# k and q of the first batch in runs of nine tokens, q's landmarks by products with a 0/1 matrix, and q turned behind the landmark scores

## The chip, the core and the metric

One core of a Trainium2 chip runs the kernel: TensorE (products), VectorE, ScalarE, GpSimd (POOL) and the DMA queues of SyncE (SP) and POOL. The metric is the device time of one execution in microseconds. The kernel before takes 811.49 us, the median of three runs from 810.85 to 811.83.

## The reference

Attention by landmarks, then two feed-forward layers. For each batch (4) and head (8), with S = 576 tokens, D = 64 and m = 32 landmarks of 18 tokens each:

```python
q_lm = q.reshape(B, H, m, S // m, D).mean(axis=3)
k_lm = k.reshape(B, H, m, S // m, D).mean(axis=3)
A, Bm, C = sm(q, k_lm), sm(q_lm, k_lm), sm(q_lm, k)      # softmax of scaled scores
Z = Bm.T / (norm1(Bm) * norminf(Bm) + 1e-06)
for _ in range(6):
    Z = 2 * Z - Z @ Bm @ Z
x = A @ Z @ C @ v                                        # (B, H, S, D) -> (2304, 512)
h = x @ w_in;  g = max(h, 0) + alpha * min(h, 0);  y = g @ w_out
h = y @ w_in2; g = h * clip(h + 3, 0, 6) / 6;      out = g @ w_out2
```

The weights arrive as 64-bit floats and are made 32-bit in the kernel. The tolerance asks for float32 accuracy, so many products run in three passes over a high and a low part.

## The kernel before, in words

The program has three parts. The **opening** computes the attention of batch 0 by itself. The **main loop** runs the first layer over eight blocks of tokens (two of each batch), 16 steps of 128 hidden features each, with the attention of the next batch and the conversion of weights between them. The last part runs the second layer over three blocks of tokens.

In the opening the order on TensorE, VectorE, ScalarE and SP is the order of the program text (`manual_schedule(engines=set(first))`, line 763); each engine takes its instructions in that order and waits for what each needs. In the main loop only TensorE and SP are ordered by hand, and a scheduler places the rest.

The order of the opening is written out in `attention(b, bank, lat, early, ...)` with `lat` = 0:

- Lines 317 to 330: SP issues k (`load_long`), q and v. `load_long` (line 251) makes one transfer of the last 64 tokens of all heads (64 partitions, runs of 256 bytes) and then `parts` transfers of the first 512 tokens (128 partitions, four tokens or 1 KB a run). k and q have four parts of two heads each. Then `early(0)` issues the first weights.
- `transposed_long` (line 294): for each pair of heads, products with the identity turn the tokens into columns, one ScalarE copy brings 512 columns to SBUF, and VectorE sums 18 columns at a time into a landmark (line 312). k goes through it first, then q. `kT` and `qT` hold the turned k and q, `kT[:, :, S:]` and `qlm` the landmarks; `bdk` is k's landmarks as a block matrix.
- `compared` (line 354): products of q's landmarks with k and k's landmarks, halves of the columns, for even and odd heads (`g`). `most_b`, `exp_b`, `most_c`, `bias_c`, `exp_c`: maxima on VectorE and exponentials on ScalarE, for B and C.
- `blocks`, `norms`: B normalised and its norms. `turned_c`, `turned_rest`: C's exponentials turned. `product`: C times v, into `x0` beside B.
- `scores` (line 428): A's scores for two tiles of tokens, in three parts: products, maximum, subtraction with exponential. `normalised` and `turned` finish A.
- `inverse` (line 503): six iterations. In each, 16 small products, a ScalarE copy and a VectorE sum, whose results the next iteration's products read. Behind each iteration the list `fill` names what else is issued there. A number n stands for `early(n)` and `joins(1)`. `warm(n)` puts n filler products on TensorE, whose results nobody reads.
- `early` (line 741) takes pieces of weights: ScalarE converts the high and the low words of a piece (`words_of`, line 195), 256 columns at a time for the first 16 pieces of `w_in`, then 512 columns of `w_out`, where POOL takes the low words. `joins` puts the two together on VectorE (`joined`, line 212).
- Line 783 on: `project(0, 0, ...)` multiplies the attention's last factor `bd` into the first weights, in two halves, and splits the result. With it the main loop can start. `emitted` counts the pieces that are begun, and the main loop's `LEAD` (line 1137) follows from it: `max(2, emitted[0] + 1)`, with `emitted[0]` the words of `w_out` begun.

A PSUM bank is taken by `bank(...)` from a ring of six in the opening, or by `two(...)` from a ring of two; a product that writes a bank waits until the bank's last reader is done.

## Time and profile before

| | us |
|---|---|
| median of 3 runs (lowest, highest) | 811.49 (810.85, 811.83) |
| the profiled execution: time, and span from first to last instruction | 808.85, 807.0 |
| busy in the span: TensorE, VectorE, ScalarE, POOL | 789.3, 588.2, 455.4, 215.2 |
| the opening, up to the start of the first projection | 37.53 |
| granted clock of TensorE over the span | 1.000 of 2.4 GHz |

Times are microseconds from the first instruction. PE is TensorE's products, PEld its weight loads, DVE is VectorE, ACT ScalarE. A product in 32-bit floats appears as two instructions. "Busy" of PE includes the filler products; products are pipelined and the ends of theirs are modelled. L307 is line 307 of the kernel, and `tp<-ident,rk` says that `tp` was written from `ident` and `rk`.

### The profile page before, as it was taken

How to read it: one execution, taken by the hardware profiler on the slowest of the kernel's cores; microseconds unless marked ns; L12 is line 12 of the kernel's file. 1: busy time of each engine (PE TensorE's matmuls, PEld its weight loads, DVE VectorE, ACT ScalarE, POOL GpSimd, SP SyncE). 2: the span in 40 equal slices, each digit the busy share in tenths (PEclk: the TensorE clock that was granted, in tenths of full speed). 3: DMA queues.
4: the chain of work that ended last, by engine and by line, in shares of the span. 5: the costliest groups of instructions: out<-in, count | busy, mean ns of one | idle time of the engine just before them, and what ended most of it. 6: DMA issues, size and time to landing. Idle time of an engine off the chain costs nothing.

```text
span 807.0 us, 16974 instructions
## 1 busy us (share of the span) xinstructions
PE 789.3 (98%) x6439; PEld 734.3 (91%) x6439; DVE 588.2 (73%) x1198; ACT 455.4 (56%) x987; POOL 215.2 (27%) x291
## 2 busy tenths in 40 slices
PE   9898998999999999999999999999999999999997
PEld 5476897888989989899999999999999999999997
DVE  4797776678856779566895587994677994677962
ACT  4785455676556676566773455752455741555541
POOL 0555003253423533344650232000223000322000
PEclk9999999999999999999999999999999999999999
DMA  9999006777386974369645777777867687677761
GB/s 270 408 414 287 19 32 178 276 228 232 108 246 216 311 229 141 125 205 346 216 156 195 296 267 293 269 281 254 319 231 276 257 300 247 248 268 269 259 229 59
DMA packets 90529, 190.91 MB, mean 237 GB/s; under 512 B 37184, under 2 KB 64336, under 8 KB 83792
## 3 DMA queue, kind: packets, MB, share of 16 engines
q1 hardware_dynamic: 80912, 151.55, 54.9%
q0 software_dynamic: 9536, 38.28, 13.4%
q8 instruction: 51, 0.84, 0.4%
q14 instruction: 30, 0.25, 0.1%
HBM read 146.81 MB, written 42.99 MB: 235 GB/s over the span
## 4 chain that ended last, share of the span: by engine, by line
PE 87%; DVE 5%; ACT 3%; DMA 2%; issue 1%; SPq 0%; DVEq 0%; ACTq 0%
PE acc L134 21%; PE l L134 20%; PE qa L1090 15%; PE h L134 12%; PE qb L1090 7%; PE acc L845 2%; PE wp L698 2%; PE tp L283 2%; PE sa L435 2%; PE sc L359 1%; PE psr L510 1%; DMA raw<-in_moe_w_in_dram 1%; DMA yr<-y_d 1%; ACT raw L202 1%; DMA rk<-in_k_dram 1%
## 5 line engine op out<-in xcount | busy, mean ns | idle before, releaser
L134 PE MATMUL acc<-gs,wout 128*128 128x288 f32 (+1 forms) x1344 | 205.4, 299 | 0.0
L134 PEld LDWEIGHTS acc<-gs,wout 128*128 128x128 f32 x1344 | 186.0, 188 | 3.1 <-issue 1.3
L134 PE MATMUL l<-yf,st 128*128 128x384 f32 x1008 | 175.5, 336 | 0.1
L134 PEld LDWEIGHTS l<-yf,st 128*128 128x128 f32 x1008 | 174.6, 188 | 0.5 <-DVE g L1037 0.5
L1090 PE MATMUL qa<-st,s 128*128 128x256 f32 x1008 | 147.3, 282 | 0.0
L1090 PEld LDWEIGHTS qa<-st,s 128*128 128x128 f32 x1008 | 132.1, 191 | 0.0
L134 PE MATMUL h<-a,w 128*128 128x288 f32 (+2 forms) x768 | 129.6, 304 | 1.7 <-DVE t L827 1.1
L128 ACT CAST s<-g 128x384 fp32r<-128x384 f32 x168 | 84.4, 512 | 79.1 <-PE qb L1090 51.2
L134 PEld LDWEIGHTS h<-a,w 128*128 128x128 f32 x768 | 108.5, 188 | 19.3 <-issue 4.4
L129 DVE TENSOR_TENSOR s<-g,s 128x384 fp32r<-128x384 f32 x168 | 88.9, 555 | 19.3 <-ACT s L128 16.4
L904 POOL TENSOR_TENSOR raw<-raw 128x128 f32<-128x128 f32 x128 | 73.6, 587 | 85.3 <-DMA raw<-in_moe_w_in_dram 34.8
L1051 POOL TENSOR_TENSOR p<-p,p 128x384 f32<-128x384 f32 x24 | 26.5, 1105 | 235.9 <-ACT p L1046 235.9
L1090 PE MATMUL qb<-st,s 128*128 128x256 f32 x504 | 87.4, 282 | 0.0
L827 DVE SCALAR_TENSOR_TENSOR t<-t,beta,h 128x288 f32<-128x288 f32 (+1 forms) x112 | 57.7, 515 | 34.7 <-ACT t L826 34.0
L826 ACT ACTIVATE t<-h 128x288 f32<-128x288 f32 (+2 forms) x120 | 49.6, 414 | 58.8 <-PE h L134 57.9
L1090 PEld LDWEIGHTS qb<-st,s 128*128 128x128 f32 x504 | 72.0, 191 | 0.0
L129 DVE TENSOR_TENSOR gs<-t,gs 128x288 fp32r<-128x288 f32 (+1 forms) x112 | 56.0, 500 | 19.8 <-ACT gs L128 19.5
L128 ACT CAST gs<-t 128x288 fp32r<-128x288 f32 (+1 forms) x112 | 48.9, 437 | 27.9 <-DVE t L827 26.5
L908 POOL DMA_DIRECT2D w_d<-fb x32 | 21.2, 661 | 66.9 <-DVE fb L129 37.7
L206 POOL TENSOR_SCALAR raw<-raw 128x512 int32<-128x512 uint32 x16 | 29.5, 1842 | 26.9 <-DMA raw<-in_moe_w_out_dram 26.0
L1036 ACT ACTIVATE ta<-l,three 128x384 f32<-128x384 f32 x24 | 14.0, 582 | 38.4 <-PE l L134 35.2
L845 PE MATMUL acc<-gs,raw 128*128 128x256 f32 x128 | 31.7, 385 | 0.0
(206 smaller groups left out, 1034.8 us busy)
## 6 DMA issues: line engine op xcount, KB each, us to landing
st<-w_d SPq DMA_DIRECT2D x48, 896.0 KB, 6.0
st<-w_d SPq DMA_DIRECT2D x42, 1024.0 KB, 5.9
w_d<-fb POOLq DMA_DIRECT2D x32, 512.0 KB, 4.1
w_d<-fa POOLq DMA_DIRECT2D x32, 384.0 KB, 3.3
raw<-in_moe_w_in_dram SPq DMA_DIRECT2D x16, 512.0 KB, 10.7
raw<-in_moe_w_out_dram SPq DMA_DIRECT2D x16, 512.0 KB, 11.3
raw<-in_moe_w_in_dram SPq DMA_DIRECT2D x64, 128.0 KB, 4.8
raw<-in_moe_w_out_dram SPq DMA_DIRECT2D x64, 128.0 KB, 4.6
```

The costliest lines, as they stand in the source:

```text
L128: nc.scalar.copy(hi, src),
L129: rest.tensor_tensor(out=lo, in0=src, in1=hi.bitcast(F32), op=ALU.subtract),
L134: nc.tensor.matmul(ps, lhsT=lhs(x), rhs=rhs(y), start=first and i == 0, stop=last and i == 2, **kw)
L206: nc.gpsimd.tensor_scalar(out=low, in0=low.bitcast(U32), scalar1=0.9374 * 2.0 ** -29, scalar2=None, op0=ALU.mult)
L283: nc.tensor.transpose(ps[:, j, :n], raw[:n, t, j * P:(j + 1) * P], ident[:n, :n])
L826: nc.scalar.activation(out=t, in_=h, func=AF.Relu, scale=-1.0),
L827: nc.vector.scalar_tensor_tensor(out=gs[:, 0] if plain else t, in0=t, scalar=beta[:, kk:kk + 1], in1=h, op0=ALU.mult, op1=ALU.add),
L845: nc.tensor.matmul(acc, lhsT=words[kk][:, ms], rhs=gs[:, 0], start=at_ == 0, stop=at_ == NK - 1)
L904: nc.gpsimd.tensor_tensor(out=y[:, o], in0=p, in1=q_, op=op)
L908: nc.gpsimd.dma_start(out=to, in_=f.bitcast(F32))
L1051: nc.gpsimd.tensor_tensor(out=p7, in0=p7, in1=p5, op=ALU.add)
L1090: nc.tensor.matmul(to[t], lhsT=s[:, y, t * P:(t + 1) * P], rhs=w[:, kp % 4, :, z], start=kp == 0 and m == 0 and t != 1, stop=kp == NU - 1 ...
```

## The change

k and q of batch 0 come by `load_runs`: each head's 576 tokens lie over 64 partitions, nine tokens (2304 bytes) in each, and two pairs of heads share the 128 partitions. A transfer brings two heads to one half of the partitions; there are four each for k and q. `turned_run` turns three of the nine tokens of two pairs of heads by six products with the identity, and `placed` copies them to their columns, which lie nine apart. k is turned that way at once, with every second copy on VectorE, and its landmarks are summed in two sums over 1152 columns. q's landmarks come from products of q with `windows`, a matrix of zeros and ones whose column l has ones at the two partitions that hold landmark l's 18 tokens; nine products for each pair are summed in PSUM, and one ScalarE copy brings all to SBUF. q itself is turned later: one half behind the landmark scores, the other half around C's product with v, the last third of that half behind the first iteration. A's first scores move into the iterations, the scores and maxima are ordered by even and odd heads, and there are fewer fillers. Pieces of weights in the iterations and just ahead of them: 12, where there were 15. `rs6` takes the buffer of `eb`.

```diff
+    HP = P // 2
+    RUN = S // HP
...
+    windows = const.tile([P, 2 * M], F32, name="windows")
+    nc.vector.tensor_reduce(
+        out=windows, in_=ident.rearrange("p (c r) -> p c r", r=W // RUN), op=ALU.add, axis=AX.X
+    )
...
+    def load_runs(src, b, nm):
+
+        raw = sb.tile([P, NTI * H * D], F32, tag="raw", name=nm, bufs=2)[:, :NP * RUN * D]
+        raw = raw.rearrange("p (i g c) -> p i g c", i=2, g=NG)
+        for i in range(2):
+            for a in range(2):
+                h = NG * (2 * i + a)
+                nc.sync.dma_start(
+                    out=raw[a * HP:(a + 1) * HP, i], in_=src[b, h:h + NG].rearrange("g (p t) d -> p g (t d)", t=RUN)
+                )
+        return raw.rearrange("p i g (t d) -> p i g t d", t=RUN)
...
-        def transposed_long(raw, xt, lm):
...
+        def both_g(ps, raw, i, t, rhs, **kw):
+            for g in range(NG):
+                nc.tensor.matmul(ps[64 * g:64 * g + 64], lhsT=raw[:, i, g, t], rhs=rhs, **kw)
+
+        def turned_run(raw, i, x, ps):
+            for t in range(3):
+                both_g(ps[:, t * P:(t + 1) * P], raw, i, 3 * x + t, ident, start=True, stop=True)
+            return ps
+
+        def placed(xt, i, x, ps, copy):
+            to = xt[:, 2 * i:2 * i + 2, :S].rearrange("q a (p t) -> q t a p", t=RUN)
+            copy(to[:, 3 * x:3 * x + 3], ps[:, :3 * P].rearrange("q (t a p) -> q t a p", t=3, a=2))
...
-            raws["k", b] = load_long(k, b, "rk", NP)
+            raws["k", b] = load_runs(k, b, "rk")
...
-        rq = load(q, b, "rq") if lat else load_long(q, b, "rq", NP)
-        turn = transposed if lat else transposed_long
+        rq = (load if lat else load_runs)(q, b, "rq")
...
-        for _ in turn(raws["k", b], kT, kT[:, :, S:]):
-            yield True
-        if lat:
+            rk = raws["k", b]
+            for i in range(2):
+                for x in range(3):
+                    placed(kT, i, x, turned_run(rk, i, x, bank("tp")), nc.vector.tensor_copy if x == 1 else nc.scalar.copy)
+                nc.vector.tensor_reduce(
+                    out=kT[:, 2 * i:2 * i + 2, S:],
+                    in_=kT[:, 2 * i:2 * i + 2, :S].rearrange("p a (l r) -> p a l r", r=W), op=ALU.add, axis=AX.X,
+                )
...
-        for _ in turn(rq, qT, qlm):
-            yield True
...
+            lm = bank("lm")
+            for i in range(2):
+                for t in range(RUN):
+                    both_g(lm[:, i * 2 * M:(i + 1) * 2 * M], rq, i, t, windows, start=t == 0, stop=t == RUN - 1)
+            nc.scalar.copy(qlm, lm[:, :NP * M].rearrange("p (j l) -> p j l", j=NP))
...
-            for hf in (1, 0):
-                for g in range(NG):
+            for g in range(NG):
+                for hf in range(2):
                     compared(g, hf)
-            a0 = scores([0, 1])
-            next(a0)
-            most_b(range(NG))
             for g in range(NG):
+                most_c(g, 0)
+                most_b([g])
+                most_c(g, 1)
+                bias_c(g)
                 exp_b(g)
-            for g in range(NG):
-                most_c(g, 1)
-                most_c(g, 0)
-                bias_c(g)
                 exp_c(g)
+            q0 = [turned_run(rq, 0, x, (two, two, bank)[x]("tp")) for x in range(3)]
             blocks()
-            warm(3)
             turned_c(0)
             norms()
             turned_c(1, nc.vector.tensor_copy)
             turned_rest()
+            for x in range(3):
+                placed(qT, 0, x, q0[x], nc.scalar.copy)
             c_scale()
-            drain(product())
+            q1 = [turned_run(rq, 1, 0, two("tp"))]
+            product_ = product()
+            next(product_)
+            q1.append(turned_run(rq, 1, 1, two("tp")))
             consts()
-            warm(6)
-            next(a0)
+            for x in range(2):
+                placed(qT, 1, x, q1[x], nc.scalar.copy)
             early(1)
+            a0 = scores([0, 1])
             n0, t0 = normalised([0, 1]), turned([0, 1])
             early(1)
             joins(1)
-            fill = [[2, a0], [2, 1], [2, n0], [1, n0], [2, 1], [t0, 1], [1]]
+            fill = [[2, 1], [a0, 2], [a0, 1, a0], [1, n0], [n0, 1], [t0, 1], [1]]
             for i, _ in enumerate(inverse()):
+                if i == 0:
+                    placed(qT, 1, 2, turned_run(rq, 1, 2, bank("tp")), nc.scalar.copy)
...
-                warm((5, 5, 4, 4, 3, 3, 6)[i])
+                warm((3, 1, 4, 4, 3, 3, 6)[i])
```

## Rows read from the trace of the kernel before

**Rows 1.** The page: busy time and share of the span of each engine.

```profile
PE 789.3 (98%) x6439; PEld 734.3 (91%) x6439; DVE 588.2 (73%) x1198; ACT 455.4 (56%) x987; POOL 215.2 (27%) x291
```

**Rows 2.** Busy time by stage: stretch, its length, busy time of each engine, clock, DMA.

```profile
25.30:38.40 13.10, 11.88 (x151) 5.24 (x150) 9.88 (x29) 10.92 (x37) 8.38 (x5) 1.00 1.02 406
41.60:55.10 13.50, 12.73 (x86) 10.28 (x87) 12.97 (x26) 12.49 (x24) 7.70 (x5) 1.00 1.02 413
55.10:67.50 12.40, 10.77 (x78) 8.48 (x77) 12.23 (x32) 9.03 (x19) 9.83 (x6) 1.00 1.08 375
```

**Rows 3.** The chain of waits, opening: start, length, what held the end.

```profile
3.20 5.57 DMA rk<-in_k_dram
...
10.62 3.71 PE tp L307 x64
14.35 0.59 ACT qT L311
...
14.97 0.77 DVE qlm L312
...
30.16 0.32 ACT raw L202
```

**Rows 4.** TensorE's timeline, from A's first scores to the first projection: start, length.

```profile
16.95 2.00 PE L435 MATMUL sa<-bdk,qT 128*128 128x64 f32 x16
...
23.94 1.47 PE L767 MATMUL idle<-idle 128*128 128x512 bf16 x6
25.34 0.53 PE L510 MATMUL psr<-nx 32*32 32x96 f32 x16
...
37.53 0.79 PE L698 MATMUL wp<-win,bd 64*32 64x256 f32 x16
```

**Rows 5.** k's transfers in the first 20 us: the first issue, all landings.

```profile
L258 SPq DMA_DIRECT2D rk<-in_k_dram x1: 750/750/750, 0.7 to 0.7; - x1
...
DMA to landing us min/median/max: 3.0/3.2/5.6
```

**Rows 6.** Table by stage, transfers: the last two columns are DMA share and GB/s.

```profile
7.20:8.20 1.00, 1.00 (x20) 0.84 (x18) 0.80 (x2) 0.64 (x2) 0.00 (x0) 1.00 1.23 199
9.00:10.40 1.40, 1.40 (x21) 1.09 (x19) 0.75 (x1) 0.57 (x2) 0.00 (x0) 1.00 1.09 348
11.00:12.50 1.50, 1.50 (x32) 1.50 (x30) 0.51 (x2) 0.59 (x1) 0.58 (x2) 1.00 1.22 179
17.00:25.00 8.00, 7.38 (x120) 5.39 (x118) 5.72 (x24) 4.67 (x19) 0.00 (x0) 1.00 1.03 410
```

**Rows 7.** Durations: two rows of TensorE's timeline, then groups by line (busy, mean ns).

```profile
10.55 3.77 PE L307 MATMUL tp<-ident,rq 128*64 128x128 f32 x64
55.83 0.68 PE L435 MATMUL sa<-bdk,qT 128*64 128x64 f32 x8
...
L202 ACT ACTIVATE raw<-raw 128x256 f32<-128x256 f32 x15 | 6.5, 435 | 0.0
...
L311 ACT COPY qT<-tp 128x512 f32<-128x512 f32 x4 | 2.3, 587 | 1.8 <-PE tp L307 1.8
L300 ACT COPY qT<-tp 128x256 f32<-128x256 f32 x1 | 0.4, 378 | 0.0
L443 DVE TENSOR_TENSOR epc<-sa,ma 128x512 f32<-128x512 f32 x1 | 0.7, 684 | 0.0
L444 ACT ACTIVATE epc<-epc 128x512 f32<-128x512 f32 x1 | 0.6, 613 | 0.0
```

**Rows 8.** Weight loads of TensorE that waited, 38.8 to 70 us; POOL's waits there.

```profile
42.25 0.11 PEld L767 LDWEIGHTS <-idle 128*128 128x128 bf16 x2 [1.11 <-DVE w L129]
...
47.62 0.77 PEld L134 LDWEIGHTS h<-a,w 128*128 128x128 f32 x6 [0.84 <-DVE raw L217]
...
67.42 0.20 PEld L465 LDWEIGHTS atp<-ident,epc 64*128 64x128 f32 x2 [1.84 <-issue]
...
POOL raw L206 <- DMA raw<-in_moe_w_out_dram: 8.4, 4, 3.7
```

## What I expect, and why

> **What bounds the kernel now.** The page comes first: TensorE is busy for 98% of the span [rows 1], so work taken off another engine is worth something only where TensorE waits. The table by stage says where that is: from 25.3 to 38.4 us TensorE shows 11.88 of 13.1 us, but much of that is filler products, and ScalarE has 10.92; from 41.6 to 67.5 us VectorE is busy for 0.96 to 0.99 of the time and ScalarE for 0.93, then 0.73 [rows 2]. The change touches the opening alone, and everything behind about 70 us is a queue of products that starts later or earlier as a block. So the question is when the opening hands over. The chain of waits gives its order: k lands at 8.77, q is turned until 14.33, copied until 14.94, and its landmarks are summed until 15.74 [rows 3]. From there a chain of scores, exponentials, C's product with v and six iterations leads to the first projection at 37.53 [rows 4].
>
> I count from 15.74, the end of q's landmarks, and sum against the profiled execution: 807.0 of span and 1.85 around it, 808.85. It stands 2.64 under the median of 811.49, so the sum's difference is put on the median. A measurement tells a difference from none at about 0.2%, 1.6 us.
>
> **The transfers.** Before, k and q came in ten transfers (two tails of 256-byte runs, eight of 1 KB runs). After, eight, each of 64 partitions x 2 heads x 2304 bytes = 294,912 bytes. SP issues two fewer, and the transfers behind them keep their order. No row shows a transfer to half the partitions in long runs, so I bound it. The first transfer, 131,072 bytes, was issued at 0.73 and landed 3.0 us later [rows 5]; at about 0.2 MB per us it moved for 0.65, so the first byte's way and receipt end at 3.1, and the n-th new transfer lands at 3.1 plus n times its duration. Best: the 410 GB/s of the weights' 4 KB runs over all partitions [rows 6], 0.72 each, last q at 8.9. Worst: half of it, 205 GB/s, 1.44 each, last q at 14.6. The nearest rows are the two stretches in which a 64-partition tail was in flight, 199 and 179 GB/s against 348 between them [rows 6]. Their packets are small, so they are no proof, but they lie at the bad end.
>
> The Trainium skill, SBUF — State Buffer, section "Can I just issue two DMAs to hit both halves?", speaks against the change: partitions 0 to 63 reach only half of the DMA's ports, and two transfers, one to each half, gain 6% over one. Its figure of 196 GB/s for 64 partitions would make 1.50 us of each, an estimate, and 1.4 us more in the sum below; the rate of rows 6 for long runs would make it 2.8 less. The low rates beside the tails agree with the page, as far as they go.
>
> **Until q's landmarks are there.** k's turning is 2 x 9 x 2 = 36 products. Each is two instructions (64 stood for the 32 before), at 3.77/64 = 0.059 us [rows 7]: 4.25 us. The landmark products of q are again 36, with the same weight load of 64 columns and half the columns streamed; the row with that load and 64 columns is 0.68 for 8, (0.68 - 0.27)/7 = 0.059 [rows 7]. So 4.25 again, where q's turning cost 3.77 and 0.46. Behind the last product stand 0.27 of its tail and one copy of about 0.27, instead of a copy of 0.59 and a sum of 0.77 [rows 3]. If the transfers are fast, TensorE sets the time: it starts when k's first half is in, 3.1 + 2 x 0.72 = 4.5, and ends at 4.5 + 8.5 + 0.5 = 13.5, a gain of 2.2. If they are slow, the last half of q sets it: 14.6 + 2.1 + 0.5 = 17.2, a loss of 1.5. I take three quarters of the way to the slow end, by the tails' rows: **+0.6**. k's two sums over 1152 elements (about 1.4 by the 0.68 that VectorE takes for 512, rows 7) and its six copies run while TensorE works on q, so they cost nothing; without that cover the second sum's 1.4 would stand on the path. The new sum for the 0/1 matrix stands in VectorE's idle time at 2 us, and costs nothing either.
>
> **From there to the first iteration.** Maxima and exponentials go head pair by head pair now; I count no gain from that, because the norms' chain of small operations stands behind both orders. What is paid: ScalarE now copies three groups of q, 384 columns each. Between 0.38 for 256 and 0.59 for 512 [rows 7] that is 0.48, or 0.39 from start to start. The fourth group of 12 instructions (0.71) needs the bank that the first copy frees, and stands ahead of C's product on TensorE: 0.48 + 0.71. Behind the product another 0.71 stands where six fillers stood, 1.47 [rows 4]: -0.76. So the first iteration's product, 25.34 - 15.74 = 9.6 behind the landmarks before [rows 4], moves to 10.0: **+0.4**.
>
> **In the iterations.** ScalarE's queue decides here: a weight piece is two conversions, 0.32 each from start to start, 0.65 [rows 3], and each iteration's small copy stands behind those ahead of it. Step by step, as differences of the distance from one iteration's product to the next:
> first to second: two copies of q (0.78) join the two pieces ahead of the evacuation, and the six fillers no longer cover that, +1.1;
> second to third: a copy (0.39) and three pieces, for two pieces and the exponential (0.61), +0.5;
> third to fourth: two pieces for three, -0.65;
> fourth to fifth: maximum 0.68, join, subtraction 0.68 and exponential 0.61 [rows 7] now stand in one chain ahead of the copy; about 2.6 for 1.6, +1.0;
> fifth to sixth: sum and reciprocal of A, +0.45.
> **+2.4** in all. Fifteen pieces were converted ahead of the first projection, twelve are after. The 16 products of A's scores move from under the exponentials into the second iteration; their 2.0 [rows 4] lies beside ScalarE's copy and three pieces, 2.3, and would stand on the path without them. The scratch that takes eb's buffer costs nothing, since eb's last reader is ten microseconds back by then.
>
> **Behind the start.** The three pieces, 3 x 0.65 = 1.95 of ScalarE, go where it has 12.49 of 13.5 us busy [rows 2]: between 0 and 1.95, I take the middle, **+1.0**. In that lies, too, that no word of w_out is begun in the opening any more, so that the lead falls from three words to two and VectorE joins each word right behind POOL. On the other side TensorE's loads wait there four times, for VectorE's or ScalarE's backlog: 1.11, 0.84, again 0.84, and 1.84 [rows 8], 4.6 in all. Conversions follow landings, and POOL waited 8.4 us for weights there [rows 8]; a later start meets more of them done. Between 0 and 4.6; I take the last wait and a little, **-1.9**, because the other three stand behind projections that move with the start.
>
> **Sum:** 0.6 + 0.4 + 2.4 + 1.0 - 1.9 = +2.5: 811.35 in a profiled execution, 814.0 as a median. The copies write with a step of nine words; the nearest rows are conversions with a step of two words, 0.435 for 256 against 0.378 for a plain copy [rows 7], so at the worst some 0.08 on each of six copies, +0.5. The likeliest case's own range goes from 813.0, with transfers halfway between their ends (-0.35 for +0.6), to its far end, rival 3.
>
> **Rivals.**
> 1. Full rate, and no more. The transfers run like those to all partitions, because consecutive ones go to different halves. For it: only small packets were seen slow. Sum: -2.2 + 2.8 + 1.0 - 1.9 = -0.3, 811.2, no difference that can be measured.
> 2. Full rate, and the weights behind come sooner too, the side of faster. With q in at 8.9, where TensorE still turned it until 14.33 [rows 3], each weight tile behind it in SP's queue lands some four microseconds sooner; POOL's 8.4 us of waits go, VectorE joins sooner, and all four of TensorE's waits vanish: -2.2 + 2.8 + 1.0 - 4.6 = -3.0, 808.5. It decides from where the gains ahead of the landmarks and in these waits exceed 3.8 + 1.6 = 5.4 together. Against it: between 41.6 and 55.1 ScalarE is full by its own work [rows 2], which landings don't shorten.
> 3. Slow transfers and nothing absorbed, the far end of the forecast: 1.5 + 2.8 + 1.95 + 0.5 = +6.8, 818.3. For it: rows 6; against it: TensorE's wait of 1.84.
>
> **How the numbers follow.** The forecast with its far end has 0.50, rival 1 has 0.28, rival 2 has 0.22. So slower 0.50, same 0.28, faster 0.22. The range goes from 809.0, which leaves out about half of rival 2, to 817.5, which leaves out the far end.
>
> **What would show it.** Right: q's last transfer lands at 13 to 14.6 with about 200 GB/s while k and q come; the copy of q's landmarks ends near 16.3; the first and second iteration's products stand 2.7 apart; the first projection starts near 41. Wrong: 350 GB/s and more ahead of 9 us (rival 1 or 2); the landmark products at under 0.04 us each; iterations as close as before, because ScalarE's copies find idle time; or, with a late first projection, TensorE's wait at 67 gone and the later blocks on time.

## The result, and the profile after

The changed kernel takes 817.04 us (median of 6 executions, 815.04 to 820.5), the kernel before 811.09 beside it (810.49 to 811.83): ratio 1.0087, 95% interval 1.007 to 1.0104 (the quotient of the two medians is 1.0073). It is slower by 5.95 us, where +2.5 was forecast. The profiled executions stand 816.03 against 808.85, spans 814.2 against 807.0, so +7.2 there; the terms below are taken from these two. Executions of one kernel differ by up to 6.6 us (the kernel before, 808.82 to 815.39 in one session), in part with the mean of their granted clock (0.992 to 1.0), which is why a median and a profiled execution are kept apart here.

The page's first part [rows 1] shows nothing: TensorE's busy time has moved by 0.3 us.

```profile
PE 789.6 (97%) x6502; PEld 737.2 (91%) x6502; DVE 588.2 (72%) x1196; ACT 457.9 (56%) x988; POOL 212.0 (26%) x291
```

The table by stage of the changed kernel, from its own marks (stretch, length, busy time of each engine, clock, DMA share and GB/s) [rows 2, 6]:

```profile
5.00:10.00 5.00, 3.83 (x36) 3.86 (x38) 0.85 (x1) 0.85 (x1) 0.00 (x0) 1.00 1.04 227
...
26.45:42.01 15.56, 12.85 (x158) 6.89 (x157) 10.48 (x29) 11.72 (x35) 10.08 (x7) 1.00 1.03 409
```

While k and q come, the transfers move 227 GB/s. The stretch from the first iteration's product to the first projection took 12.19 us before (25.34 to 37.53, rows 4); it takes 15.56, and TensorE, ScalarE and VectorE all show idle time in it.

The chain of waits of the opening (start, length, what held the end) [rows 3]:

```profile
5.45 8.46 DMA rq<-in_q_dram
14.04 1.28 PE lm L314 x36
...
22.22 0.75 ACT qT L323
23.02 0.88 PE tp L314 x12
...
26.14 1.43 ACT qT L323 x2
...
29.50 0.50 ACT qT L323
```

q's last transfer now holds the chain until 13.91, the landmark products follow in 1.28, and three times ScalarE's copies of q stand in the chain. TensorE's timeline [rows 4], the six iterations' products and the first projection:

```profile
26.45 0.83 PE L532 MATMUL psr<-nx 32*32 32x96 f32 x16
...
29.35 0.57 PE L532 MATMUL psr<-nx 32*32 32x96 f32 x16 [0.50 <-ACT nx L559]
...
32.54 0.53 PE L532 MATMUL psr<-nx 32*32 32x96 f32 x16 [0.48 <-DVE nx L562]
...
33.97 0.53 PE L532 MATMUL psr<-nx 32*32 32x96 f32 x16
...
36.55 0.53 PE L532 MATMUL psr<-nx 32*32 32x96 f32 x16 [1.08 <-DVE nx L562]
...
38.31 0.53 PE L532 MATMUL psr<-nx 32*32 32x96 f32 x16 [0.47 <-DVE nx L562]
...
42.01 0.79 PE L725 MATMUL wp<-win,bd 64*32 64x256 f32 x16
```

Before, these stood at 25.34, 26.99, 29.23, 31.28, 32.84, 34.06 and 37.53. The first comes 1.11 us late, the projection 4.48: three quarters of that arise inside the iterations. Two groups by line between 5 and 42 us (busy, mean ns) give the price of what was added:

```profile
L323 ACT COPY qT<-tp 128x384 f32<-128x384 f32 x6 | 4.6, 879 | 0.0
...
L314 PE MATMUL lm<-windows,rq 128*64 128x64 f32 x72 | 2.5, 223 | 0.7 <-DMA rq<-in_q_dram 0.7
```

And the weight loads that waited behind the start [rows 8]:

```profile
46.73 0.11 PEld L794 LDWEIGHTS <-idle 128*128 128x128 bf16 x2 [1.11 <-DVE w L131]
...
52.49 0.77 PEld L136 LDWEIGHTS h<-a,w 128*128 128x128 f32 x6 [0.85 <-DVE gs L854]
55.85 0.30 PEld L136 LDWEIGHTS h<-a,w 128*128 128x128 f32 x2 [1.04 <-ACT w L130]
...
73.51 0.20 PEld L487 LDWEIGHTS atp<-ident,epc 64*128 64x128 f32 x2 [1.84 <-issue]
```

The waits of 1.11, 0.84 and 1.84 of before are all still there, and one of 1.04 for ScalarE is new. The load at 73.51 stood at 67.42: +6.09. From there the same VectorE operations of both kernels, set side by side, are +6.09 at 118 us of before, +5.04 at 157, about that until 570, and +7.1 at the end. So 1.05 comes back between 118 and 157, where TensorE was busy for 35.89 of 40 us before and is for 37.46 now (by stage):

```profile
120.00:160.00 40.00, 37.46 (x410) 31.96 (x409) 27.41 (x59) 24.16 (x56) 11.56 (x18) 1.00 0.57 174
```

The last 2.07 is a wait far behind the change (TensorE's timeline, then VectorE's):

```profile
587.74 2.53 PE L136 MATMUL l<-yf,st 128*128 128x384 f32 x13 [2.07 <-DVE g L1064]
```
```profile
581.02 0.96 DVE L996 TENSOR_TENSOR t<-yr 128x768 f32<-128x768 f32 x1 [1.91 <-DMA yr<-y_d]
```

A transfer of y landed 8.6 us behind its issue, 7.1 before. This is hardly the change's own: the same wait is 0.7 to 1.4 us in the profiles of seven of the twelve kernels below, and 0.2 or less in the other five. Of the kernel before there is one profile, without it, so that it never has this wait is not shown.

### The profile page after: what moved, and what is told of

It reads as the page before. It is cut to its first block, busy times and chain, and to the rows that moved or that the text cites. A ratio compares the mean times of both kernels' runs of the same rounds, so it can differ in the third digit from the quotient of the medians.

```text
span 814.2 us, 17094 instructions
## 1 busy us (share of the span) xinstructions
PE 789.6 (97%) x6502; PEld 737.2 (91%) x6502; DVE 588.2 (72%) x1196; ACT 457.9 (56%) x988; POOL 212.0 (26%) x291
## 4 chain that ended last, share of the span: by engine, by line
PE 86%; ACT 4%; DVE 4%; DMA 3%; issue 1%; SPq 1%; DVEq 0%; ACTq 0%
PE acc L136 20%; PE l L136 20%; PE qa L1117 15%; PE h L136 12%; PE qb L1117 7%; PE acc L872 3%; PE wp L725 2%; PE sa L457 2%; PE tp L301 2%; DMA raw<-in_moe_w_in_dram 1%; DMA yr<-y_d 1%; ACT raw L208 1%; DMA rq<-in_q_dram 1%; PE sc L381 1%; PE psr L532 1%
## 5 line engine op out<-in xcount | busy, mean ns | idle before, releaser
L131 DVE TENSOR_TENSOR gs<-t,gs 128x288 fp32r<-128x288 f32 (+1 forms) x112 | 55.8, 498 | 19.6 <-ACT gs L130 19.1
L212 POOL TENSOR_SCALAR raw<-raw 128x512 int32<-128x512 uint32 x16 | 27.0, 1687 | 23.0 <-DMA raw<-in_moe_w_out_dram 22.1
```

What stands on the lines that cost most here:

```text
L131: rest.tensor_tensor(out=lo, in0=src, in1=hi.bitcast(F32), op=ALU.subtract),
L212: nc.gpsimd.tensor_scalar(out=low, in0=low.bitcast(U32), scalar1=0.9374 * 2.0 ** -29, scalar2=None, op0=ALU.mult)
```

## The experiments

The theory after reading both traces: the loss is (a) transfers that fill half of the partitions, (b) copies of q with single columns nine words apart, (c) work moved into the iterations, where ScalarE takes its work in the order of the program. The rivals: the late start is of no account because it is taken up later, or the moved weight pieces cost it. All edits are to the changed kernel unless said otherwise, each timed in five rounds beside before, whose medians were 811.48, 810.64, 810.55 and 810.67 in the four sessions.

### 1. Transfers over all partitions

```diff
-            for a in range(2):
-                h = NG * (2 * i + a)
-                nc.sync.dma_start(
-                    out=raw[a * HP:(a + 1) * HP, i], in_=src[b, h:h + NG].rearrange("g (p t) d -> p g (t d)", t=RUN)
+            pairs = src[b, 2 * NG * i:2 * NG * (i + 1)].rearrange("(a g) (p t) d -> g p a (t d)", a=2, t=RUN)
+            for g in range(NG):
+                nc.sync.dma_start(out=raw[:, i, g], in_=pairs[g])
...
-        out=windows, in_=ident.rearrange("p (c r) -> p c r", r=W // RUN), op=ALU.add, axis=AX.X
+        out=windows.rearrange("q (a l) -> q a l", a=2), in_=ident.rearrange("q (l r a) -> q a l r", a=2, r=W // RUN), op=ALU.add, axis=AX.X
...
-                both_g(ps[:, t * P:(t + 1) * P], raw, i, 3 * x + t, ident, start=True, stop=True)
+                both_g(ps[:, t * P:(t + 1) * P], raw, i, 3 * x + t, ident.rearrange("q (p a) -> q a p", a=2), start=True, stop=True)
```

> Edit: the run of tokens p of the pair's two halves goes to neighbouring partitions 2p and 2p+1, so that each of the eight transfers of k and q fills all 128 partitions with the same 294,912 bytes in the same packets; the 0/1 matrix and the identity are read in the matching order. Theory 'half the partitions, half the rate': the transfers land about 0.85 us apart (the 348 GB/s of before's best stretch) instead of 1.3, q's last landing goes from 13.9 us to 10.5 to 11.5, qlm's copy ends 2 to 3 us sooner (12.6 to 13.6 instead of 15.6), and as the iterations hang on that copy by the chain of waits, the time falls by 1.5 to 3 us, to about 815. Rival 'the packet's size': the packets keep their 2304 bytes, so they land 1.3 us apart as before and the time stays at 817. Rival 'covered': the landings come sooner but the products of k at the half clock (0.107 us each) and the weight pieces set the pace, and less than 0.5 us is left of it at the first projection.

Measured: 814.39 us, ratio to before 1.0038 [1.0023, 1.0053]. The first 10 us by stage, and TensorE's timeline:

```profile
5.00:10.00 5.00, 4.89 (x73) 4.65 (x72) 2.18 (x3) 2.61 (x3) 0.00 (x0) 1.00 0.89 309
```
```profile
24.54 0.76 PE L530 MATMUL psr<-nx 32*32 32x96 f32 x16
...
39.89 0.79 PE L723 MATMUL wp<-win,bd 64*32 64x256 f32 x16
```

The same 2304-byte pieces move at 309 GB/s instead of 227; q's last transfer lands at 12.03 instead of 13.91, the first iteration comes 1.91 sooner, the first projection 2.12, and the median falls by 2.65. So the half-filled transfers are worth about 2 us of the loss, and the piece's size is not the cause. The landings vary from one execution to the next: q's landmarks are there at 14.89 to 15.89 us in the five profiles of this order with half-filled transfers, and at 12.84 to 14.42 in the four with full ones, so the 2 us of this one pair can be off by about 1 us. The last rival speaks of a half clock for k's first products; they did follow each other at half the rate, but the profile's clock column there is 1.00. The Trainium skill, SBUF — State Buffer, section "Can I just issue two DMAs to hit both halves?", says that only one transfer that spans all partitions reaches all ports; the two rates agree with it in direction.

### 2. Copies of three columns at a time

```diff
-                both_g(ps[:, t * P:(t + 1) * P], raw, i, 3 * x + t, ident, start=True, stop=True)
+                both_g(ps[:, t:3 * P:3], raw, i, 3 * x + t, ident, start=True, stop=True)
...
-            to = xt[:, 2 * i:2 * i + 2, :S].rearrange("q a (p t) -> q t a p", t=RUN)
-            copy(to[:, 3 * x:3 * x + 3], ps[:, :3 * P].rearrange("q (t a p) -> q t a p", t=3, a=2))
+            to = xt[:, 2 * i:2 * i + 2, :S].rearrange("q a (p t) -> q a p t", t=RUN)
+            copy(to[:, :, :, 3 * x:3 * x + 3], ps[:, :3 * P].rearrange("q (a p t) -> q a p t", t=3, a=2))
```

> Edit: the products that turn k and q write every third column of the bank, so that the copies read the bank in a row and write three tokens side by side (12 bytes of every 36) instead of single columns 36 bytes apart. Theory 'the copies pay for the scattered columns': a copy of 128x384 falls from 0.85 to between 0.48 and 0.65 us, the first iteration's product comes 0.6 to 1.0 us sooner than 26.45, the second another 0.3, and the time falls by about 1.2 us to 815.8. Rival 'any written gap costs the same': copies stay at 0.85, time unchanged at 817. Rival 'the gap moves to TensorE': copies get cheaper, but the products that write every third column take longer than the 0.027 to 0.06 us of now.

Measured: 817.44 us, 1.0078 [1.0054, 1.0101]. The group of the copies, TensorE's timeline, and three stretches by stage:

```profile
L323 ACT COPY qT<-tp 128x384 f32<-128x384 f32 x6 | 2.9, 548 | 0.0
```
```profile
25.43 0.37 PE L532 MATMUL psr<-nx 32*32 32x96 f32 x8
...
40.37 0.79 PE L725 MATMUL wp<-win,bd 64*32 64x256 f32 x16
```
```profile
69.60:73.00 3.40, 1.64 (x13) 1.37 (x13) 3.40 (x9) 1.55 (x4) 0.00 (x0) 1.00 0.14 22
73.00:76.40 3.40, 3.40 (x9) 2.70 (x9) 1.65 (x4) 0.27 (x1) 0.59 (x1) 0.50 0.68 148
```

The copies are cheaper as the theory said, 0.548 us each instead of 0.879. TensorE pays nothing for writing every third column (both forms: 278 ns mean for q's products, 0.88 us for a group of twelve). The Trainium skill, SBUF — State Buffer, section "Door 1: The DMA port swizzle", in its note on "cachelines", says that each step to a new 16-byte line costs; 12 of every 36 bytes against 4 of every 36 agrees with it in direction. The first iteration comes 1.02 sooner and the first projection 1.64, but 0.72 of both is an earlier landing of q in this execution (13.19 against 13.91), which the edit does not touch. Counted from q's landmarks, the first iteration comes after 10.54 us instead of 10.84 and the iterations take 14.94 instead of 15.56: the copies' form is worth 0.3 and 0.6 us there. The time did not fall. At the third turning, the load that stood at 73.51, 0.81 of the lead of 1.64 was left (72.70). Behind the stretch in which TensorE waited there (1.64 busy of 3.40) its granted clock stood at 0.50, that is 1.2 of 2.4 GHz, for 3.4 us, and behind that the same VectorE operations come 0.87 later than in the changed kernel. Five of this kernel's six executions had a mean clock of 0.997 or less, four of the changed kernel's six 0.999.

### 3. Both

```diff
-                both_g(ps[:, t * P:(t + 1) * P], raw, i, 3 * x + t, ident, start=True, stop=True)
+                both_g(ps[:, t:3 * P:3], raw, i, 3 * x + t, ident.rearrange("q (p a) -> q a p", a=2), start=True, stop=True)
```

(and the other lines of 1 and 2)

> Edit to the changed kernel: transfers over all partitions and copies in groups of three tokens together. Theory 'two separate terms': qlm's copy ends near 13.4 us, the first iteration's product comes at 23.3 to 23.8, the first projection at 38.2 to 38.6 (42.01 less 2.1 and 1.6), and without a fall of the clock the time is 812.5 to 813.5. Rival 'one covers the other': the copies are no longer on the path once k lands sooner, and the first projection stays at 39.5 or later, the time at 814.

Measured: 813.42 us, 1.0042 [1.0026, 1.0058]. The first projection stands at 40.35, not at 38.2 to 38.6; q's last transfer landed later in this profiled execution than in the first experiment (12.81 against 12.03). From q's landmarks to the first projection it is 25.93 us, against 26.25 in the first experiment, 25.48 in the second and 26.40 in the changed kernel: with full transfers the copies' form gives 0.3 where it gave 0.9 alone. The time is inside what "two separate terms" gave, the marks of the trace are not, so the two terms add up only in part.

### 4. The new load alone, in the order of before

```diff
-            raws["k", b] = load_long(k, b, "rk", NP)
+            raws["k", b] = load_runs(k, b, "rk")
...
+            for i in range(2):
+                for x in range(3):
+                    placed(xt, i, x, turned_run(raw, i, x, bank("tp")), nc.vector.tensor_copy if x == 1 else nc.scalar.copy)
+                nc.vector.tensor_reduce(
+                    out=lm[:, 2 * i:2 * i + 2],
+                    in_=xt[:, 2 * i:2 * i + 2, :S].rearrange("p a (l r) -> p a l r", r=W), op=ALU.add, axis=AX.X,
+                )
```

(an edit to the kernel before; q is loaded the same way)

> Edit: the kernel before with the new load alone: k and q in runs of nine tokens, turned by the new products and copies, but q's landmarks summed by VectorE from the turned q and the opening in the order of before, with all 15 pieces. Theory 'the load costs the start of the landmarks, the moved turning of q costs the rest': q's last landing at 13.9 us, then products, a copy of 0.85 and a sum of about 1.3 us give q's landmarks at 17 to 17.5 us instead of 15.74 (+1.3 to +1.8); from there on all runs as before, 9.6 us to the first iteration and the iterations as close as before, so the time is 812.3 to 813.3, clearly under the changed kernel. Rival 'all of the loss is the load': the time is 817 or more. Rival 'covered': the first projection's +1.5 is recovered at the third atp, where before waits 1.84 us, and the time is 811.

Measured: 816.88 us, 1.0069 [1.0044, 1.0094]. TensorE's timeline, then a stretch by stage:

```profile
18.21 1.65 PE L374 MATMUL sc<-kT,qlm 64*32 64x320 f32 x28 [1.66 <-DVE qlm L326]
...
30.14 0.53 PE L525 MATMUL psr<-nx 32*32 32x96 f32 x16
```
```profile
18.90:25.70 6.80, 6.80 (x45) 5.18 (x29) 3.32 (x14) 2.71 (x12) 0.00 (x0) 0.50 1.03 411
```

The first iteration comes 4.80 late, where 1.3 to 1.8 was expected. Taken alone this would have said "all of the loss is the load". But TensorE waited 1.66 us for the late landmarks, and from 18.9 its granted clock stood at 0.50 for 6.8 us in which it was busy throughout. So one more run:

```diff
         for _ in turn(rq, qT, qlm):
             yield True
+        warm(7)
```

> Edit to the kernel with the new load alone (order of before): seven filler products after the last turning of q, where TensorE waited 1.66 us for the landmarks before its granted clock stood at 0.5 from 18.9 to 25.7 us. Theory 'the load alone costs about 2.4 us, the clock the other 2.5': the granted clock stays at 1.0 between 17 and 30 us, the products of the opening go back to their lengths of before, the first iteration's product comes at 27.3 to 27.9 instead of 30.14, and the time falls by 2 to 2.5 us to 814.5. Rival 'the clock falls all the same or the path is VectorE's sums': the first iteration stays within 0.5 us of 30.1 and the time at 816.9.

Measured: 813.97 us, 1.0038 [1.002, 1.0055]. TensorE's timeline, then its weight loads:

```profile
15.67 1.68 PE L783 MATMUL idle<-idle 128*128 128x512 bf16 x7
...
27.63 0.53 PE L526 MATMUL psr<-nx 32*32 32x96 f32 x16
```
```profile
39.83 0.79 PE L714 MATMUL wp<-win,bd 64*32 64x256 f32 x16
```
```profile
69.80 0.20 PEld L481 LDWEIGHTS atp<-ident,epc 64*128 64x128 f32 x2 [1.84 <-issue]
```

With the wait filled, the clock stays at 1.00 in the opening, the first iteration comes 2.51 sooner, and the median stands 3.3 us over that of before beside it instead of 5.4. What is left is the load's own price: 2.29 at the first iteration, 2.30 at the first projection, 2.38 at the third turning, 2.4 in the span (this profiled execution is the fastest of its twelve; the medians give 3.3). This run bears on the step on absorption as well: from the first iteration on only the start was moved, and TensorE's wait at the third turning is 1.84 as before. It also gives the price of the other part: here, with the order of before, the iterations take 12.20 us (27.63 to 39.83), in the changed kernel 15.56.

### 5. The load mended, in the order of before

The last kernel with the edits of 1 and 2, of which this is the line that holds both:

```diff
-                both_g(ps[:, t * P:(t + 1) * P], raw, i, 3 * x + t, ident, start=True, stop=True)
+                both_g(ps[:, t:3 * P:3], raw, i, 3 * x + t, ident.rearrange("q (p a) -> q a p", a=2), start=True, stop=True)
```

> Edit: the kernel with the new load alone, in the order of before with the seven fillers, and besides it the full transfers and the copies grouped by three tokens. Theory 'the load is dear only by its half-filled transfers and scattered copies': q's last landing near 12 us, the last copy 0.3 us shorter, q's landmarks at 15.2 to 16.2 us (before: 15.74), the first iteration's product at 24.8 to 25.8 (before: 25.34), the time within 0.7 us of before, 810.4 to 811.8. Rival 'runs of nine cost besides': the landmarks wait for a whole half of q (sum of 1.35 us over 1152 elements in a row), the first iteration stays above 26.3 and the time above 812.

Measured: 813.68 us, 1.0042 [1.0027, 1.0057]. VectorE's timeline, then TensorE's:

```profile
15.32 1.35 DVE L324 TENSOR_REDUCE qlm<-qT 128x64 f32<-128x1152 f32 x1 [0.17 <-ACT qT L317]
```
```profile
26.30 0.53 PE L524 MATMUL psr<-nx 32*32 32x96 f32 x16
```

q lands at 12.06, and still the landmarks come at 16.67, 0.93 late: the rival "runs of nine cost besides". A half of q is 36 products and one sum of 1.35 us over 1152 elements in a row, where before a quarter of it was followed by 0.77. The median, 3.1 over before, is worse than the opening (+1.04 at the first projection), and the profiled execution shows part of the reason in its case: +1.72 at the third turning, then a granted clock of 0.50 from 69.4 to 72.8.

### 6. Three weight pieces back in the opening

```diff
-            fill = [[2, 1], [a0, 2], [a0, 1, a0], [1, n0], [n0, 1], [t0, 1], [1]]
+            fill = [[2, 1], [a0, 2], [a0, 1, a0], [2, n0], [n0, 2], [t0, 2], [1]]
```

> Edit: three of the weight pieces that the change took out of the opening are put back, one each in iterations 4, 5 and 6 (15 pieces as before instead of 12). Theory 'the moved pieces cost 1.4 us': in the opening ScalarE has waits of 1.2, 0.3 and 1.6 us in these iterations, so the first projection comes no more than 0.5 us after 42.01, and the step from +4.48 to +5.88 us between the first and the second projection is gone; the time falls by about 1 us to 816. Rival 'they cost as much in front': each piece's 0.33+0.33 us on ScalarE delays its iteration, the first projection comes 1 to 2 us later and the time stays at 817 or rises.

Measured: 816.6 us, 1.0067 [1.0044, 1.009]; beside the changed kernel's 1.0087 no difference that can be told. TensorE's timeline, then its weight loads:

```profile
42.76 0.79 PE L725 MATMUL wp<-win,bd 64*32 64x256 f32 x16
```
```profile
55.98 0.42 PEld L136 LDWEIGHTS h<-a,w 128*128 128x128 f32 x3 [0.38 <-DVE w L131]
...
70.66 0.20 PEld L487 LDWEIGHTS atp<-ident,epc 128*128 128x128 f32 x2 [1.23 <-DVE w L131]
...
73.64 0.20 PEld L487 LDWEIGHTS atp<-ident,epc 64*128 64x128 f32 x2 [1.84 <-issue]
```

The new wait of 1.04 for ScalarE is gone, as the first theory said, but the first projection comes 0.75 later and the third turning at 73.64 instead of 73.51. As q's landmarks were 0.36 sooner here, the pieces cost 1.10 us in the iterations (16.66 instead of 15.56), 0.37 each. Behind the first projection only 0.62 comes back (30.88 to the third turning, 31.50 in the changed kernel, 29.89 before), because TensorE now waits 1.23 for VectorE at 70.66, where it waited 0.48. So in front the pieces are no cheaper than behind.

### 7. Three of q's late copies on VectorE

```diff
-                placed(qT, 0, x, q0[x], nc.scalar.copy)
+                placed(qT, 0, x, q0[x], nc.vector.tensor_copy if x == 1 else nc.scalar.copy)
```

(the first and the last copy of the second half likewise)

> Edit to the changed kernel: three of the six late copies of q (the second of the first half, the first and the last of the second half) go to VectorE, which waits 3.2, 1.3 and 1.6 us in this stretch, instead of ScalarE. Theory 'ScalarE in order is what spreads the first iterations': the wait of TensorE for the copy of qT (1.2 us) shrinks to under 0.7, the first iteration's product comes 0.5 to 0.8 us sooner than 26.45, the gap from first to second iteration falls from 2.9 to about 2.2 us, and the first projection comes 1.0 to 1.8 us sooner than 42.01; the time falls to 815 to 816. Rival 'VectorE is next': the copies delay VectorE's own steps of the iteration (L554, L562) by as much, and the first projection stays within 0.4 us of 42.0. Rival 'given back later': the first projection is sooner, but ScalarE's full stretch from 50 to 60 us holds the second projection where it was.

Measured: 817.89 us, 1.0093 [1.0069, 1.0116]. A stretch by stage, and TensorE's timeline:

```profile
22.90:26.30 3.40, 3.40 (x90) 2.44 (x84) 0.51 (x4) 0.21 (x1) 0.00 (x0) 0.50 1.02 404
```
```profile
23.60 2.82 PE L516 MATMUL pu<-v,ct 128*32 128x64 f32 x80
```

Inconclusive for the time: the clock fell in just this stretch, C's product took 2.82 us instead of 1.73, and the first iteration came at 27.32. From it to the first projection the kernel takes 14.47 us instead of 15.56, so ScalarE's order is part of the spread. The same three copies on VectorE in the kernel of 3:

```diff
-                    placed(qT, 1, 2, turned_run(rq, 1, 2, bank("tp")), nc.scalar.copy)
+                    placed(qT, 1, 2, turned_run(rq, 1, 2, bank("tp")), nc.vector.tensor_copy)
```

> Edit: as the one with full transfers and grouped copies, and the three late copies of q on VectorE besides. Theory 'three separate terms': the first projection comes at 37.0 to 37.6, as before the change (37.53), and what is left over the kernel before is the price of the three moved weight pieces at the second projection, about 1 us: 811.5 to 812.5. Rival 'VectorE is next': no further gain over the one without it, 813.

Measured: 813.05 us, 1.0025 [1.0009, 1.004], the best of these kernels and still slower than before. TensorE's timeline, then its weight loads:

```profile
23.45 0.51 PE L530 MATMUL psr<-nx 32*32 32x96 f32 x10
...
37.97 0.79 PE L723 MATMUL wp<-win,bd 64*32 64x256 f32 x16
```
```profile
69.91 0.20 PEld L485 LDWEIGHTS atp<-ident,epc 64*128 64x128 f32 x2 [1.84 <-issue]
```

The three edits bring the first projection from 42.01 to 37.97, 0.44 behind before, with q's landmarks at 12.84, 2.9 ahead of before. But the iterations still take 14.52 us, and at the third turning +0.44 has become +2.49. That this is what ScalarE no longer does ahead of the first projection and has to do behind it is argued, not shown: experiment 6 gave back 0.62 of it. Whether the pieces, put back into this kernel, would change that was not tried.

### 8. Landmark products in the order of before

Edits 1 and 2 and the products with the 0/1 matrix in the kernel before: q's first half turned between the two halves' landmark products, its second half behind the landmark scores, 15 pieces, all fillers.

```diff
+            lm = bank("lm")
+            for i in range(2):
+                for t in range(RUN):
+                    both_g(lm[:, i * 2 * M:(i + 1) * 2 * M], rq, i, t, windows, start=t == 0, stop=t == RUN - 1)
+                if i == 0:
+                    for x in range(3):
+                        placed(qT, 0, x, turned_run(rq, 0, x, bank("tp")), nc.vector.tensor_copy if x == 1 else nc.scalar.copy)
+            nc.scalar.copy(qlm, lm[:, :NP * M].rearrange("p (j l) -> p j l", j=NP))
...
                     compared(g, hf)
+            for x in range(3):
+                placed(qT, 1, x, turned_run(rq, 1, x, bank("tp")), nc.scalar.copy)
             a0 = scores([0, 1])
```

> Edit: order, fillers and all 15 weight pieces of before, with the full transfers and grouped copies, q's landmarks by the products with the 0/1 matrix, q's first half turned as it lands and its second half right behind the landmark scores, where ScalarE waits 2.2 us for the first exponential's input. Theory 'the landmark products are worth what T gains, once nothing is moved into the iterations': qlm ends at 12.8 to 13.6 us, the first iteration's product comes at 22.6 to 23.8 us (before 25.34), the first projection at 34.8 to 36.2 (before 37.53), and the gain is kept: the time is 808.5 to 809.8, below both kernels. Rival 'something else then sets the iterations' (weight pieces or v land too late for an earlier start): the first projection gains under 0.7 us, the time is 810.3 or more. Rival 'the clock': a wait of TensorE in the opening brings a granted clock of 0.5 for some microseconds, and the time is above 811.

Measured: 816.06 us, 1.0071 [1.0053, 1.0088]: a miss. TensorE's timeline, then ScalarE's:

```profile
13.73 1.27 PE L312 MATMUL lm<-windows,rq 128*64 128x64 f32 x34
```
```profile
18.45 1.23 ACT L321 COPY qT<-tp 128x384 f32<-128x384 f32 x2 [3.15 <-PE tp L312]
```

In TensorE's order the second half's landmark products stood behind 2.2 us of turning, so the landmarks came at 15.31; and the second half's copies reached ScalarE only at 18.45, ahead of the exponentials in its order. The first iteration came at 28.58, and from 71.4 to 78.2 the granted clock stood at 0.50 besides. The gain of the landmark products depends on nothing standing ahead of them or behind them in these two queues; the experiment says nothing against the products themselves.

### 9. Fillers back

```diff
             blocks()
+            warm(2, bank)
             turned_c(0)
...
             turned_rest()
+            warm(4, bank)
```

> Edit to the changed kernel: two filler products ahead of the first turning of the exponentials and four behind the last one, where TensorE waits 0.7, 0.5 and 1.2 us (the change took out three fillers and six at about these places). Theory 'without the fillers the clock falls in some executions': no execution has a mean granted clock of 0.993 or less by a fall in the opening, the highest time comes down from 820 to 818 and the median by 0.5 to 1 us, to 816 to 816.5. Rival 'falls come at the third turning of the scores near 72 us': the spread stays as it is, 815 to 820, median 817. Rival 'the fillers lie on the path': the first projection comes 0.3 us or more later than 42.0.

Measured: 815.67 us, 1.0057 [1.0038, 1.0077], whose interval meets the changed kernel's. Five of six executions have a mean clock of 0.999 or more; the profiled one does not, with 0.53 from 16.0 to 19.6 and 0.51 from 40.0 to 43.5, both away from the fillers; its first projection, at 44.76, says nothing on their price for that reason. The same two lines in the kernel of 813.05 us:

> Edit: the best of the versions in the order of the change (full transfers, copies grouped by three tokens, three late copies on VectorE) with the two groups of filler products of the warm one added. Theory 'the rest over before is the moved weight pieces, 1.5 us at the second projection, and falls of the clock in some executions': fewer executions have a mean granted clock under 0.998 than the 4 of 12 without the fillers, the median falls from 813.05 to 811.8 to 812.5, the lowest stays near 810. Rival 'the fillers change nothing': 813.0 with the same spread. Rival 'it beats before': a median under 810.5 would mean that nothing of the moved pieces arrives at the end.

Measured: 814.13 us, 1.0043 [1.0025, 1.006]: not better than 1.0025, and five of twelve executions have a clock under 0.998, three of twelve without (not four, as the expectation has it). So fillers at these two places are of no use that these runs can show. No version beat the kernel before.

## Why the forecast was wrong

The direction was right and so were the first mark (slow transfers, q's last landing at 13 to 14.6: 13.91) and the shape of the iterations. The size was off by 4.7 us in the profiled execution, 3.5 in the median. What failed first of all is the step "behind the start": 1.9 us were to be absorbed at TensorE's waits, and none was there. Next come an overlap that was lost ahead of the first iteration (step 2) and the price of the scattered copies (step 3). That the median is still inside the stated range (809.0 to 817.5) is luck in part, because the landmark products erred the other way. By the steps:

1. **Until q's landmarks: +0.6 forecast, -0.13 measured** (15.61 for 15.74). The transfers came as forecast, at 227 instead of about 200 GB/s. The landmark products were mis-sized: taken at 0.059 us an instruction from a row with the same weight load, they took (1.28 - 0.22)/35 = 0.030, so that only 1.7 us stand behind the last transfer. That error went in the change's favour, and it is one of the prediction's own signs of being wrong (under 0.04 us each). What the half-filled transfers took back is about 2 us, by the first experiment.
2. **To the first iteration: +0.4 forecast, +1.24 measured** (10.84 for 9.60). The sum of a copy, the fourth group of turning and the fillers left out an overlap. Before, the first forty of C's products ran while VectorE still copied the turned exponentials (ct), and only the second forty waited for it. After, TensorE's order puts the fourth group, which waits for ScalarE's first copy of q, ahead of all eighty. TensorE's timeline before, after, and in experiment 2 (`tp` is that group, `pu` C's product):

```profile
21.78 0.90 PE L494 MATMUL pu<-v,ct 128*32 128x64 f32 x40
22.95 0.90 PE L494 MATMUL pu<-v,ct 128*32 128x64 f32 x40 [0.27 <-DVE ct L478]
```
```profile
23.02 0.88 PE L314 MATMUL tp<-ident,rq 128*64 128x128 f32 x12 [1.20 <-ACT qT L323]
23.83 1.73 PE L516 MATMUL pu<-v,ct 128*32 128x64 f32 x80
```
```profile
22.81 1.73 PE L516 MATMUL pu<-v,ct 128*32 128x64 f32 x80
```

From q's landmarks, the first copy's end costs only 0.20 more than the wait of before (7.41 for 7.21), the group 0.81, the first half of C's product, now on the path, 0.82, and the absent fillers give back 0.59 of the 0.76 forecast. The copies' size is the smaller part: at 0.548 us each, near the 0.48 forecast, the distance is still 10.54 to 10.62 (experiments 2, 3 and 7). No run puts that group behind C's product, so this split is read from the rows.

3. **In the iterations: +2.4 forecast, +3.37 measured** (15.56 for 12.19). The distances were forecast as +1.1, +0.5, -0.65, +1.0, +0.45 and came as +1.25, +0.95, -0.62, +1.02, +0.54, and 0.23 more ahead of the projection. The two that miss most are those with copies in them, and here the copies' size is the term that failed: 0.48 us from rows of contiguous copies, with 0.08 more at the worst for the step of nine words, where they took 0.879. The nearest row, a step of two words, was no bound for a step of nine. With copies of 0.548 the same two distances came as +0.97 and +0.53 (experiment 2), close to the forecast. That the order of the work sets the iterations is shown: the order of before restores 12.20 under the same load. ScalarE's queue is a part of that, as three copies moved to VectorE take 1.1 and 0.8 us off (experiment 7), and the rest stays open.
4. **Three pieces: +1.0 forecast, +1.61 measured** (6.09 at the third turning less 4.48). Inside its bounds of 0 to 1.95. Only part of it is shown to be the pieces' price: put back, they returned 0.62 here and cost 1.10 in front.
5. **Absorbed: -1.9 forecast, none at the waits named.** This is the step that failed in kind. I read four waits of TensorE as backlog of VectorE and ScalarE that a later start would meet done. All four are there after the change, and with only the start moved by 2.3 us they stand at the same lengths; the one of 1.84 is 1.84 or 1.85 in all fourteen profiles. Two of them can be followed in the rows: the first is for VectorE's `w`, made from the product `wp` that TensorE has just written, and the last for VectorE's `a`, made from TensorE's own last turning `atp` (timeline of the kernel before):

```profile
66.90 0.74 DVE L129 TENSOR_TENSOR a<-atp,a 128x256 fp32r<-128x256 f32 x2
...
67.45 0.31 PE L465 MATMUL atp<-ident,epc 64*128 64x64 f32 x2 [1.63 <-DVE a L129]
```

TensorE waits for an operation that waits for it, so the wait moves along. What did come back, 1.05 us, came between 120 and 160 us, at no place that I named.

6. **A wait at 587 us, +2.07**, was in no step. It follows a late transfer of y and comes and goes between these kernels.

Together -0.13 + 1.24 + 3.37 + 1.61 - 1.05 + 2.07 = +7.1, the profiled difference. Of the rivals the third, slow transfers and nothing absorbed, named the two conditions that held, with other terms in it (818.3). Rivals 1 and 2 fell with the transfers' rate; experiment 1 shows that with transfers to all partitions (309 GB/s, not the 410 of these rivals) the time is still 0.38% above before, so the landings alone do not bring what the two rivals name.

## What to carry to other kernels

Price a copy by its write pattern: look for a row with the same step, and where none exists let the bound be a factor, not a few hundredths; and load into all partitions at once, since neighbouring half transfers on one queue did not make up for each other here (227 against 309 GB/s). Before work is put ahead of a product, look which part of that product ran inside a wait: that part comes onto the path too. A wait in the profile is slack for a late start only if what it waits for does not itself hang on the waiting engine: follow its releaser back one round before counting it as slack. And where an edit makes TensorE wait, read the granted clock behind that wait before putting the loss down to the edit.

## What was not expected of the hardware

Columns written one by one, 36 bytes apart, cost 0.85 to 0.88 us for 384 on ScalarE and 0.83 to 0.86 on VectorE alike (of k's six copies VectorE has two, the middle one of each half, not every second one); three together 0.55 and 0.56. A product with a weight load of 64 columns and 64 columns streamed, alternating between two halves of the array's columns, followed the next after 0.03 us. A wait of TensorE of 1.7 us in the opening was followed by a granted clock of 0.50 for 6.8 us and cost 2.5 us, more than the wait; behind the wait of 1.84 us at the third turning the clock fell to 0.50 for 3.4 us in some kernels' profiled executions (6.8 us in that of experiment 8) and not in others', with the same wait in all. What decides between them stays open. In the changed kernel's profile k's first 40 product instructions took 417 ns on average against 278 for q's, under a clock column of 1.00; it cost nothing there, since TensorE waited 0.66 us for q's last transfer behind them.
